# Clears on GpSimd, table writes one by one, and scaling rows with a higher priority in a fused attention and mixture-of-experts kernel

## The chip, the cores and the metric

The kernel runs on one core of a Trainium2 chip. The metric is device time in microseconds (us); a time is that of one execution of the whole program, and where several runs are given, the median counts. The engines have these names in the profile: PE is TensorE (PEld its weight loads), DVE is VectorE, ACT is ScalarE, POOL is GpSimd, SP is SyncE, which here only issues DMAs. POOL also issues the indirect DMAs (gathers and scatters by row index).

## The reference

Causal attention over 4 batches, 8 heads, 576 positions of 64 values, mixed with a read from a memory matrix; its output is the input of a top-2 mixture of 8 experts.

```
scores = causal(scale * q @ k.T);  a = exp(scores - scores.max(-1))
a /= a.sum(-1) + 1e-09
local = a @ v
q_p = phi(q)                                   # phi(x) = max(x,0) + exp(min(x,0))
mem_out = (q_p @ M_prev) / (q_p . z_prev + 1e-06)
g = sigmoid(beta)                              # one per head
x = (g * mem_out + (1 - g) * local)            # rows: (batch, position), 512 columns

noisy_logits = x @ w_gate + log1p(exp(x @ w_noise)) * noise
top2, top2_w = two largest of 8 and their softmax
for e in range(8):  out[mask] += top2_w * (relu(x[mask] @ w1[e]) @ w2[e])     # 1024 hidden
```

## The kernel before

**Attention.** The 576 positions of a batch are cut into five chunks, four of 128 and one of 64; chunk (b, i) is number i of batch b, 20 in all. A chunk is worked off in units (two units of four heads for i < 2, else four of two heads). The main loop runs over the units, `u`, as a pipeline: scores of unit u + 2 (`score`), exponentials of u + 1 (`expo`), transposes of a (`trans`, tile tpa, copied to aT by ScalarE), and the products with v of unit u - 2 (`av`, tile avT). In a unit, the maximum over a row (nb, line 570) is a reduction on VectorE, the exponential (line 591) is on ScalarE. The preparation of later chunks (q and k transposed, split into a high and a low fp32r part on GpSimd, phi of q in qpT, the memory read xm) is slotted in between by a table of due times.

**End of a chunk.** `out_turn` makes the chunk's rows x: VectorE adds 1e-9 to the sums den and multiplies by the gate's denominator (line 659, or 664 for the chunks of 64; tile ar), takes the reciprocal (665), TensorE transposes the attention output xo into tpo (668), VectorE multiplies (670, tile xr) and adds the memory part xm (672). xr is stored to xall_scratch by SyncE (676), and `xt_logits` transposes it (line 153, tile tpx), splits it (xTlh on ScalarE, xTll on VectorE, 158) and multiplies it with the gate weights (165, 166, tile tpl; the logits lg at 173).

**Routing.** When a batch's last chunk is through, `routing` puts some forty small steps (line 199 and around) into the queue `small`, from which the loop takes one between its other steps. It ends with the tile rows, and with ten table writes (`put`, line 285): indirect DMAs on GpSimd that scatter rows to tab_scratch at the slot of each token, ten per batch. They go to the queue `puts`; the loop takes one per unit, two in the last batch. For the third batch (B - 2), `early` stands behind the routing steps as a last one: it drains `puts` at once, loads the first two experts' slots from the table (tabE, line 901, on SyncE, each waiting for all 30 writes) and gathers expert 0's first rows into xgE (three tiles of 128x512 in the buffer xw, line 857). That buffer is the one that held batch 2's keys; `early_rows` takes it over and clears the three tiles by VectorE (line 893). Later `xprep` (line 909) transposes the gathered rows.

**Experts.** From about 283 us on TensorE runs the experts' matmuls (980: ha, hb; 993: y), with weights streamed in and split in high and low parts.

**What sets the order.** A scheduling layer puts the traced instructions of each engine in one static order; `tc.high_priority(offset=n)` makes it place instructions as if they had been traced n steps sooner. `here(f)` traces f behind the last instruction of the step before on VectorE, ScalarE and GpSimd. On the chip each engine works off its order strictly, and waits by semaphores.

Of the kernel before, what the change touches and what calls it, by code (L numbers as in the profile page):

```python
# [15 lines left out]
ALU = mybir.AluOpType  # L16
# [4 lines left out]
B, H, S, D = 4, 8, 576, 64  # L21
# [4 lines left out]
NCH = 5  # L26
# [20 lines left out]
def tile_attention_moe(ctx: ExitStack, tc: tile.TileContext, q, k, v, M_prev, z_prev, beta,  # L47
# [295 lines left out]
    def attention():  # L343
        with ExitStack() as c2:
# [308 lines left out]
            def out_turn(c):  # L653

                d = CH[c]
                n = d["n"]
                r = d["r"] = ap_.tile([P, H], F32, tag="ar", name="ar", bufs=2)
                if d["i"] < 4:
                    nc.vector.scalar_tensor_tensor(out=r, in0=d["den"], scalar=1e-9, in1=il, op0=ALU.add, op1=ALU.mult)
                else:  # L660
                    rv = r[0:n].rearrange("p (g t) -> p g t", t=2)
                    lv = il[0:n].rearrange("p (g t) -> p g t", t=2)
                    for t, s_ in enumerate((d["d2"][0:64], d["xo"][0:64, 0, 64:68])):
                        nc.vector.scalar_tensor_tensor(out=rv[:, :, t], in0=s_, scalar=1e-9, in1=lv[:, :, t], op0=ALU.add, op1=ALU.mult)
                nc.vector.reciprocal(r[0:n], r[0:n])
                tp = ps_tp.tile([P, 512], F32, tag="tp", name="tpo")
                for g in range(4):
                    nc.tensor.transpose(tp[0:n, g * P:(g + 1) * P], d["xo"][:, g, 0:n], ident)
                x_ = d["x"] = rp.tile([P, H, D], F32, tag="xr", name="xr", bufs=3)
                nc.vector.tensor_tensor(out=x_[0:n], in0=tp[0:n].rearrange("p (h e) -> p h e", h=H),  # L670
                                        in1=d["r"][0:n].unsqueeze(2).to_broadcast([n, H, D]), op=ALU.mult)
                nc.vector.tensor_tensor(out=x_[0:n], in0=x_[0:n], in1=d["xm"][0:n], op=ALU.add)
                t0 = d["b"] * S + d["i"] * P

                def keep():
                    nc.sync.dma_start(out=xall[t0:t0 + n, :], in_=x_[0:n].rearrange("p h d -> p (h d)"))
                if c == len(chunks) - 1:
                    R["keep"] = keep
                    return
                keep()  # L680
                xq.extend(xt_logits(d["b"], d["i"], x_.rearrange("p h d -> p (h d)")))
                if d["i"] == 4:
                    xq.append(lambda b=d["b"]: small.extend(routing(b) + ([early] if b == B - 2 else [])))
                if d["b"] == B - 1 and d["i"] == 2:
                    xq.append(lambda: small.extend(routing(B - 1, 0, 3)))
                if d["b"] == B - 1 and d["i"] == 3:
                    xq.insert(1, lambda: xprep(R["XT0"], R["xgE"][0], 0))
                    xq.append(lambda: xprep(R["XT0"], R["xgE"][1], 1))
                    xq.append(lambda: xprep(R["XT0"], R["xgE"][2], 2))
# [81 lines left out]
            def smalls(last=False):  # L771

                for _ in range(2 if last else 1):
                    if small:
                        in_turn(small.popleft())

            for u in range(NU + 2):
                if u + 1 < NU:
                    expo(u + 1)
# [12 lines left out]
                if u < NU:  # L792
# [8 lines left out]
                    if u >= first[len(chunks) - 5] - 2 and splits:  # L801
                        xs.append(lambda f=splits.popleft(): here(f))
                        xs.append(lambda f=splits.popleft(): here(f))
                    if u == first[len(chunks) - 5] + 1:
                        xs.append(lambda: here(early_rows))
                    if chunks[c][1] == 4 and (u + 1 == NU or units[u + 1][0] != c):
                        xs.append(lambda c=c: sums(c))
                    while ev and ev[0][0] < TU[u + 1]:
# [9 lines left out]
                            pops.append(xq.popleft())  # L818
                    if len(xq) > 2:
                        pops.append(xq.popleft())  # L820
                    for _ in range(2 if chunks[c][0] == B - 1 else 1):
                        if puts:
                            xs.append(lambda: puts and here(puts.popleft()))
                    k_ = 0 if c == len(chunks) - 1 else max(0, len(pops) - 1)
                    xs += pops[:k_] + (trans(u) if u > 1 else [])
                    late_ = pops[k_:]
                nx, ny = len(xs), max(1, len(ys))
                done = 0
                late = u >= NU - 4
# [55 lines left out]
    def early_rows():  # L885

        w_ = kp.tile([P, H, S], F32R, tag="kT", name="xw").rearrange("p h s -> p (h s)")
        R["xgE"] = [w_[:, t * DM:(t + 1) * DM].bitcast(F32) for t in range(3)]
        for j in range(2):
            o = 3 * DM + j * 4 * EARLY  # L890
            R["XT0"].append(w_[:, o:o + 4 * EARLY].rearrange("p (c t) -> p c t", c=4))
        for t in range(3):
            nc.vector.memset(R["xgE"][t], 0.0)

    def early():

        while puts:
            puts.popleft()()
        assert len(scat) == 2 * NCH * (B - 1), len(scat)
        for e in range(2):  # L900
            after_puts(nc.sync.dma_start(
                out=tabE[:, e], in_=tab[e * CAP:e * CAP + EARLY].rearrange("(p t) c -> p t c", p=P)))
        for t in range(3):
            gather_x(R["xgE"][t], tabE[:, 0, t, 0:1], (B - 1) * S)
# [392 lines left out]
```

## Time and profile before

| | us |
|---|---|
| median of 3 runs | 735.73 |
| lowest, highest | 734.84, 738.34 |
| the profiled execution, its own time | 733.98 |
| its span, first to last instruction | 732.3 |

| engine | busy, us | share of the span |
|---|---|---|
| PE | 695.3 | 95% |
| PEld | 600.7 | 82% |
| DVE | 459.1 | 63% |
| ACT | 381.3 | 52% |
| POOL | 360.8 | 49% |

The profile is one execution. A timeline row gives the start, the duration, the engine, the line, what is written and read, and in brackets how long the engine had been idle and what ended that. "x8" means eight instructions in one row. A table by stretches gives for each stretch the busy time of each engine and PEclk, the share of full clock that TensorE was granted (1.00 is the upper of two levels, 0.50 the lower). Ends of matmuls are modelled, since they are pipelined.

### The profile page before, as it was taken

How to read it: one execution, taken by the hardware profiler on the slowest of the kernel's cores; microseconds unless marked ns; L12 is line 12 of the kernel's file. 1: busy time of each engine (PE TensorE's matmuls, PEld its weight loads, DVE VectorE, ACT ScalarE, POOL GpSimd, SP SyncE). 2: the span in 40 equal slices, each digit the busy share in tenths (PEclk: the TensorE clock that was granted, in tenths of full speed). 3: DMA queues.
4: the chain of work that ended last, by engine and by line, in shares of the span. 5: the costliest groups of instructions: out<-in, count | busy, mean ns of one | idle time of the engine just before them, and what ended most of it. 6: DMA issues, size and time to landing. Idle time of an engine off the chain costs nothing. (4 is left out here: it accounts for less than half of the span.)

```text
span 732.3 us, 14474 instructions
## 1 busy us (share of the span) xinstructions
PE 695.3 (95%) x5161; PEld 600.7 (82%) x5161; DVE 459.1 (63%) x1097; ACT 381.3 (52%) x963; POOL 360.8 (49%) x378
## 2 busy tenths in 40 slices
PE   7999999999979678999999999999999999999996
PEld 6788878877857567898888898898898898899895
DVE  6767687687877557968785686455454454454322
ACT  5888987878767554444564153153153153253210
POOL 5505325643762534457554676833833753723702
PEclk8999999999989989999999999999999999999999
DMA  8664422432000026769994594693693693753401
GB/s 174 143 155 132 103 59 59 99 89 55 23 10 30 2 75 173 204 180 246 234 248 132 149 238 146 177 215 110 180 211 116 173 227 121 201 151 129 131 1 63
DMA packets 173966, 98.18 MB, mean 134 GB/s; under 512 B 112852, under 2 KB 152276, under 8 KB 173888
## 3 DMA queue, kind: packets, MB, share of 16 engines
q1 hardware_dynamic: 163424, 78.20, 42.6%
q0 software_dynamic: 10080, 18.98, 9.6%
q8 instruction: 42, 0.69, 0.4%
q14 instruction: 36, 0.29, 0.2%
q10 hardware_dynamic: 384, 0.02, 0.0%
HBM read 74.41 MB, written 22.54 MB: 132 GB/s over the span
## 5 line engine op out<-in xcount | busy, mean ns | idle before, releaser
L936 POOL TENSOR_TENSOR w1lm<-w1sm,w1hm 128x512 fp32r<-128x512 f32 x72 | 93.9, 1307 | 121.0 <-DVE w1hm L939 66.5
L993 PE MATMUL y<-w2hm,hTl 128*128 128x512 f32 (+1 forms) x310 | 122.1, 394 | 0.3 <-DVE hTl L984 0.3
L993 PE MATMUL y<-w2hm,hTh 128*128 128x512 f32 (+1 forms) x310 | 122.1, 394 | 0.0
L993 PE MATMUL y<-w2lm,hTh 128*128 128x512 f32 (+1 forms) x310 | 121.4, 392 | 0.0
L983 ACT ACTIVATE hTh<-ha 128x304 fp32r<-128x304 f32 (+2 forms) x64 | 27.2, 424 | 143.0 <-PE ha L980 121.0
L940 DVE TENSOR_TENSOR w2lm<-w2sm,w2hm 128x512 fp32r<-128x512 f32 x74 | 62.2, 841 | 55.8 <-ACT w2hm L939 54.9
L939 ACT CAST w2hm<-w2sm 128x512 fp32r<-128x512 f32 x74 | 45.6, 619 | 95.9 <-PE y L993 83.3
L591 ACT ACTIVATE a<-sc,nb 128x128 f32<-128x128 f32 (+4 forms) x160 | 82.7, 529 | 11.8 <-DVE nb L570 7.4
L570 DVE TENSOR_REDUCE nb<-sc 128x1 f32<-128x384 f32 (+4 forms) x128 | 68.9, 556 | 27.8 <-PE sc L565 11.6
L939 DVE CAST w1hm<-w1sm 128x512 fp32r<-128x512 f32 x74 | 36.1, 488 | 63.3 <-PE hb L980 38.3
L993 PEld LDWEIGHTS y<-w2hm,hTl 128*128 128x128 f32 (+1 forms) x310 | 56.5, 182 | 16.5 <-DVE hTl L984 1.1
L980 PE MATMUL hb<-xTh,w1hm 128*128 128x304 f32 (+2 forms) x224 | 68.6, 306 | 0.2 <-DVE hTl L984 0.2
L980 PE MATMUL ha<-xTl,w1hm 128*128 128x304 f32 (+2 forms) x224 | 68.2, 304 | 0.0
L980 PE MATMUL hb<-xTl,w1hm 128*128 128x304 f32 (+2 forms) x224 | 68.0, 303 | 0.1
L980 PE MATMUL ha<-xTh,w1hm 128*128 128x304 f32 (+2 forms) x224 | 67.8, 303 | 0.0
L980 PE MATMUL hb<-xTh,w1lm 128*128 128x304 f32 (+2 forms) x224 | 67.7, 302 | 0.0
L980 PE MATMUL ha<-xTh,w1lm 128*128 128x304 f32 (+2 forms) x224 | 67.6, 302 | 0.0
L993 PEld LDWEIGHTS y<-w2lm,hTh 128*128 128x128 f32 (+1 forms) x310 | 56.6, 183 | 11.5
L993 PEld LDWEIGHTS y<-w2hm,hTh 128*128 128x128 f32 (+1 forms) x310 | 56.6, 183 | 10.7
L610 ACT COPY aT<-tpa 128x512 f32<-128x512 f32 x120 | 56.6, 518 | 8.4 <-PE tpa L609 4.9
L609 PE MATMUL tpa<-identr,a 128*128 128x128 f32 x400 | 58.9, 281 | 0.8 <-ACT mm L500 0.2
L631 PE MATMUL avT<-aT,vt 128*64 128x128 f32 (+1 forms) x960 | 59.5, 266 | 0.0
(252 smaller groups left out, 1645.9 us busy)
## 6 DMA issues: line engine op xcount, KB each, us to landing
w1sm<-in_moe_w_dram SPq DMA_DIRECT2D x74, 256.0 KB
w2sm<-in_moe_w_dram SPq DMA_DIRECT2D x74, 256.0 KB
y_scratch<-o SPq DMA_DIRECT2D x21, 256.0 KB
vt<-in_v_dram SPq DMA_DIRECT2D x16, 256.0 KB
xall_scratch<-xr SPq DMA_DIRECT2D x16, 256.0 KB
kn<-in_k_dram SPq DMA_DIRECT2D x15, 256.0 KB
qn<-in_q_dram SPq DMA_DIRECT2D x15, 256.0 KB
y_scratch<-o SPq DMA_DIRECT2D x14, 224.0 KB
```

The lines of the kernel that those rows point to most:

```text
L570: R["nb"] = nc.vector.tensor_reduce(out=nb[:, t * nh:(t + 1) * nh], in_=cols[t] if nh == 2 else cols[t][:, 0, :], axis=AX.X, op=ALU.max, n ...
L591: nc.scalar.activation(a[:, o:o + w], s_, AF.Exp, bias=st["nb"][:, x_:x_ + 1], accum_out=d["den"][:, at:at + 1])
L609: nc.tensor.transpose(tp[:, x_ * P:(x_ + 1) * P], a[:, (g + x_) * P:(g + x_ + 1) * P], ident)
L610: nc.scalar.copy(aT[:, g:g + w, :].rearrange("p b t -> p (b t)"), tp[:, 0:w * P])
L631: nc.tensor.matmul(o_[k_ * 64:(k_ + 1) * 64, h0 // 2, 0:n], CH[c0 + j]["v"][:, h0 + k_, :], r_, start=(j == 0), stop=(j == i))
L936: R["w1l"] = lo.tensor_tensor(out=l1, in0=a, in1=h1.bitcast(F32), op=ALU.subtract)
L939: lambda: nc.vector.tensor_copy(h1, a), l1_, lambda: nc.scalar.copy(h2, b_),
L940: lambda: nc.vector.tensor_tensor(out=l2, in0=b_, in1=h2.bitcast(F32), op=ALU.subtract)]
L980: nc.tensor.matmul(o, w_[:, c, :], xT[xi][:, c, c0_ - at:c1_ - at], start=(c == 0 and i_ == 0), stop=(c == 3 and i_ == 2))
L983: R["hh"] = nc.scalar.activation(hT[0][:, c0_:c1_], o, AF.Relu)
L993: nc.tensor.matmul(ys[t][0:b_ - a_], hT[hi][:, a_:b_], w_, start=(f == 0 and i_ == 0), stop=(f == FF // P - 1 and i_ == 2))
```

## The change

Three edits.

1. The clears of the three xgE tiles go from VectorE to GpSimd, and are traced one per unit over three units, beginning with the third unit's step of batch 3 (`clear_row`); the buffer is taken over at the first of them.
2. In `out_turn` the two small rows for ar with the reciprocal, and the product and sum that make xr, stand in `tc.high_priority(offset=240)`, for every chunk.
3. `early` is no longer a step of `small`, and no longer drains the queue. In the last batch each unit takes one table write in the middle of its steps and one at their end, as long as writes of the first three batches are left; `try_early` runs `early` once the thirtieth is traced. The writes of the earlier batches move to another place within the unit.

```diff
-                if d["i"] < 4:
-                    nc.vector.scalar_tensor_tensor(out=r, in0=d["den"], scalar=1e-9, in1=il, op0=ALU.add, op1=ALU.mult)
...
-                nc.vector.reciprocal(r[0:n], r[0:n])
+                with tc.high_priority(offset=240):
+                    if d["i"] < 4:
+                        nc.vector.scalar_tensor_tensor(out=r, in0=d["den"], scalar=1e-9, in1=il, op0=ALU.add, op1=ALU.mult)
...
+                    nc.vector.reciprocal(r[0:n], r[0:n])
...
-                nc.vector.tensor_tensor(out=x_[0:n], in0=tp[0:n].rearrange("p (h e) -> p h e", h=H),
-                                        in1=d["r"][0:n].unsqueeze(2).to_broadcast([n, H, D]), op=ALU.mult)
-                nc.vector.tensor_tensor(out=x_[0:n], in0=x_[0:n], in1=d["xm"][0:n], op=ALU.add)
+                with tc.high_priority(offset=240):
+                    nc.vector.tensor_tensor(out=x_[0:n], in0=tp[0:n].rearrange("p (h e) -> p h e", h=H),
+                                            in1=d["r"][0:n].unsqueeze(2).to_broadcast([n, H, D]), op=ALU.mult)
+                    nc.vector.tensor_tensor(out=x_[0:n], in0=x_[0:n], in1=d["xm"][0:n], op=ALU.add)
...
-                    xq.append(lambda b=d["b"]: small.extend(routing(b) + ([early] if b == B - 2 else [])))
+                    xq.append(lambda b=d["b"]: small.extend(routing(b)))
...
+            def try_early():
+
+                if "early" not in R and len(scat) == 2 * NCH * (B - 1):
+                    R["early"] = True
+                    here(early)
...
-                    if u == first[len(chunks) - 5] + 1:
-                        xs.append(lambda: here(early_rows))
+                    u_ = u - first[len(chunks) - 5] - 2
+                    if u_ == 0:
+                        early_rows()
+                    if 0 <= u_ < 3:
+                        xs.append(lambda t=u_: here(lambda: clear_row(t)))
+                    if len(scat) < 2 * NCH * (B - 1):
+                        xs.append(lambda: puts and here(puts.popleft()))
...
-                    for _ in range(2 if chunks[c][0] == B - 1 else 1):
-                        if puts:
-                            xs.append(lambda: puts and here(puts.popleft()))
...
+                    if chunks[c][0] == B - 1 and "early" not in R:
+                        xs.append(lambda: puts and here(puts.popleft()))
+                        xs.append(try_early)
...
-        for t in range(3):
-            nc.vector.memset(R["xgE"][t], 0.0)
+
+    def clear_row(t):
+        nc.gpsimd.memset(R["xgE"][t], 0.0)
...
-        while puts:
-            puts.popleft()()
```

In the rows of order that follow, the numbers behind the names tell buffers apart and differ between the two programs; the changed kernel's line numbers are larger by 1 to 14 for the same statement (ar 659, 664, 665 become 660, 665, 666; xr 670, 672 become 672, 674; the gather 857 becomes 870).

VectorE, around the end of chunk (2,4): before, from the second maximum of a unit (nb) to the sum that completes xr.

```order
L570 TENSOR_REDUCE nb_3596<-sc_3598 128x2
L940 TENSOR_TENSOR w2lb_2700<-w03_251,w2hb_2699 128x512
L893 MEMSET xw_3628 128x512 x3
L570 TENSOR_REDUCE nb_3673<-sc_3674 128x1
L504 SCALAR_TENSOR_TENSOR mr_3639<-mm_3637,ib_90 128x4
L664 SCALAR_TENSOR_TENSOR ar_3655<-xo_3611,ib_90 64x4
L489 TENSOR_SCALAR qpT_3837<-qf_3694 128x512
L506 RECIPROCAL mr_3639<-mr_3639 128x4
L665 RECIPROCAL ar_3655<-ar_3655 64x8
L670 TENSOR_TENSOR xr_3664<-tpo_3659,ar_3655 64x512
L417 SCALAR_TENSOR_TENSOR qpT_3837<-qf_3694,qpT_3837 128x512
L672 TENSOR_TENSOR xr_3664<-xr_3664,xm_3193 64x512
```

The same place in the changed kernel, from the first maximum of that unit on.

```order
L570 TENSOR_REDUCE nb_3597<-sc_3598 128x2
L665 SCALAR_TENSOR_TENSOR ar_3651<-xo_3612,ib_90 64x4
L952 TENSOR_TENSOR w2lb_2700<-w03_251,w2hb_2699 128x512
L666 RECIPROCAL ar_3651<-ar_3651 64x8
L570 TENSOR_REDUCE nb_3597<-sc_3599 128x2
L672 TENSOR_TENSOR xr_3660<-tpo_3655,ar_3651 64x512
L504 SCALAR_TENSOR_TENSOR mr_3637<-mm_3635,ib_90 128x4
L674 TENSOR_TENSOR xr_3660<-xr_3660,xm_3195 64x512
L660 SCALAR_TENSOR_TENSOR ar_3943<-den_3591,ib_90 128x8
L506 RECIPROCAL mr_3637<-mr_3637 128x4
L570 TENSOR_REDUCE nb_3669<-sc_3670 128x1
L666 RECIPROCAL ar_3943<-ar_3943 128x8
```

The clears are gone from this queue, and the sum that completes xr stands ahead of the next unit's maximum and of both rows of the q work (qpT).

GpSimd, the writes of the third batch's table rows (six_3862), before.

```order
L451 TENSOR_TENSOR kT_3283<-kf_3833,kT_3283 128x4x128
L507 TENSOR_TENSOR xm_3983<-mm_3987,mr_3989 128x256
L507 TENSOR_TENSOR xm_3983<-mm_4060,mr_4062 128x256
L285 DMA tab_scratch<-rows_89,six_3862 19456x4 x10
L857 DMA xw_3628<-xall_scratch,tabE_99 128x512 x3
```

The same in the changed kernel.

```order
L451 TENSOR_TENSOR kT_3285<-kf_3833,kT_3285 128x4x128
L507 TENSOR_TENSOR xm_3991<-mm_3995,mr_3997 128x256
L285 DMA tab_scratch<-rows_89,six_3862 19456x4 x5
L507 TENSOR_TENSOR xm_3991<-mm_4076,mr_4078 128x256
L285 DMA tab_scratch<-rows_89,six_3862 19456x4 x5
L870 DMA xw_3672<-xall_scratch,tabE_99 128x512 x3
```

The ten writes stand in two groups of five, with one row of the memory part between them.

GpSimd, where the clears (L907) stand in the changed kernel.

```order
L507 TENSOR_TENSOR xm_3560<-mm_3635,mr_3637 128x256
L907 MEMSET xw_3672 128x512
L481 CAST qh_3694<-qf_3692 128x512
L907 MEMSET xw_3672 128x512
L483 TENSOR_TENSOR ql_3695<-qf_3692,qh_3694 128x512
L507 TENSOR_TENSOR xm_3754<-mm_3758,mr_3760 128x256
L507 TENSOR_TENSOR xm_3754<-mm_3770,mr_3772 128x256
L907 MEMSET xw_3672 128x512
```

One stands ahead of each of the two rows that split q of a later chunk (qh, ql), the third behind the next two xm rows.

## Rows read from the trace of the kernel before

**Rows 1.** The page's first part: busy time, share of the span, instructions.

```profile
PE 695.3 (95%) x5161; PEld 600.7 (82%) x5161; DVE 459.1 (63%) x1097; ACT 381.3 (52%) x963; POOL 360.8 (49%) x378
```

**Rows 2.** Stretches: start:end length, busy us (instructions) per engine, PEclk, DMA share, GB/s.

```profile
211.10:216.05 4.95, 0.00 (x1) 0.03 (x1) 4.70 (x12) 1.60 (x5) 3.67 (x4) 0.95 0.00 0
216.05:222.40 6.35, 6.35 (x40) 5.27 (x41) 1.05 (x3) 3.22 (x9) 0.68 (x1) 0.50 0.12 23
...
251.30:259.64 8.34, 0.01 (x1) 0.00 (x0) 1.92 (x6) 1.22 (x3) 4.38 (x5) 0.81 0.03 2
259.64:263.40 3.76, 3.76 (x27) 3.23 (x28) 0.00 (x0) 1.52 (x6) 2.06 (x2) 0.51 0.39 105
...
300.00:730.00 430.00, 425.04 (x2426) 377.95 (x2424) 242.45 (x446) 164.44 (x317) 221.53 (x212) 1.00 0.65 166
```

**Rows 3.** Waits of PE on DVE for tpx: us in total, times, longest.

```profile
PE tpx L153 <- DVE ar L659: 5.9, 3, 5.0
```

**Rows 4.** Timeline of PE around 211 us: start, duration, row, idle before.

```profile
210.88 0.22 PE L565 MATMUL sc<-mask,identb 128*128 128x128 bf16 x1
216.05 0.66 PE L153 MATMUL tpx<-identr,xr 64*128 64x64 f32 x4 [4.95 <-DVE ar L659]
...
216.72 1.92 PE L609 MATMUL tpa<-identr,a 128*128 128x128 f32 x8
```

**Rows 5.** Timeline of DVE before 216 us.

```profile
207.66 1.26 DVE L570 TENSOR_REDUCE nb<-sc 128x2 f32<-128x512 f32 x2
209.06 0.69 DVE L940 TENSOR_TENSOR w2lb<-w,w2hb 128x512 fp32r<-128x512 f32 x1
209.81 1.57 DVE L893 MEMSET xw<- 128x512 f32 x3
...
211.77 0.15 DVE L664 SCALAR_TENSOR_TENSOR ar<-xo,ib 64x4 f32<-64x4 f32 x1
...
212.73 0.68 DVE L670 TENSOR_TENSOR xr<-tpo,ar 64x512 f32<-64x512 f32 x1
213.34 1.55 DVE L417 SCALAR_TENSOR_TENSOR qpT<-qf,qpT 128x512 f32<-128x512 f32 x1
214.81 1.09 DVE L672 TENSOR_TENSOR xr<-xr,xm 64x512 f32<-64x512 f32 x1
```

**Rows 6.** Timeline of ACT: the copy of xo.

```profile
208.34 0.17 ACT L644 COPY xo<-avT 64x4 f32<-64x4 f32 x1
```

**Rows 7.** Timelines of PE, ACT and POOL from 244 to 260 us.

```profile
250.24 1.07 PE L609 MATMUL tpa<-identr,a 128*128 128x128 f32 x8
259.64 0.32 PE L165 MATMUL tpl<-xTlh,wgs 128*32 128x128 f32 x1 [8.34 <-ACT aT L610]
...
256.84 0.58 ACT L157 CAST xTlh<-tpx 128x512 fp32r<-128x512 f32 x1 [6.88 <-remote]
...
244.65 1.02 POOL L285 DMA_INDIRECT tab_scratch<-rows,six  x1 [2.64 <-DVE rows L199]
...
256.00 0.90 POOL L285 DMA_INDIRECT tab_scratch<-rows,six  x1 [0.30 <-issue]
```

**Rows 8.** Timelines of ACT and POOL around the six writes at 282 us.

```profile
291.13 0.20 ACT L167 COPY lt<-tpl 32x64 f32<-32x64 f32 x1 [1.41 <-remote]
...
282.15 1.02 POOL L285 DMA_INDIRECT tab_scratch<-rows,six  x1 [5.56 <-DVE ar L665]
...
289.00 0.96 POOL L285 DMA_INDIRECT tab_scratch<-rows,six  x1 [0.30 <-issue]
```

**Rows 9.** PE's row at 275 us, and the stretch around it.

```profile
275.31 0.66 PE L909 MATMUL tpm<-identr,xw 128*128 128x128 f32 x4 [1.16 <-ACT aT L610]
...
270.00:280.00 10.00, 8.01 (x104) 6.35 (x105) 7.21 (x40) 6.09 (x20) 4.82 (x6) 1.00 0.57 176
```

**Rows 10.** POOL: a row after idle time, and the group of its clears (busy, mean ns).

```profile
223.61 1.19 POOL L507 TENSOR_TENSOR xm<-mm,mr 128x256 f32<-128x256 f32 x2 [6.88 <-ACT mm L500]
...
L1059 POOL MEMSET xg<- 128x512 f32 x3 | 1.6, 536 | 5.7 <-PE sc L550 5.3 <-PE tpm L497 0.4
```

More of the change, by code (lines that the diff above doesn't have):

```diff
@@ L657, in out_turn @@
                 r = d["r"] = ap_.tile([P, H], F32, tag="ar", name="ar", bufs=2)
-                if d["i"] < 4:
-                    nc.vector.scalar_tensor_tensor(out=r, in0=d["den"], scalar=1e-9, in1=il, op0=ALU.add, op1=ALU.mult)
[L660 to L664, printed above, removed]
-                nc.vector.reciprocal(r[0:n], r[0:n])
+                with tc.high_priority(offset=240):
+                    if d["i"] < 4:
+                        nc.vector.scalar_tensor_tensor(out=r, in0=d["den"], scalar=1e-9, in1=il, op0=ALU.add, op1=ALU.mult)
+                    else:
+                        rv = r[0:n].rearrange("p (g t) -> p g t", t=2)
+                        lv = il[0:n].rearrange("p (g t) -> p g t", t=2)
+                        for t, s_ in enumerate((d["d2"][0:64], d["xo"][0:64, 0, 64:68])):
+                            nc.vector.scalar_tensor_tensor(out=rv[:, :, t], in0=s_, scalar=1e-9, in1=lv[:, :, t], op0=ALU.add, op1=ALU.mult)
+                    nc.vector.reciprocal(r[0:n], r[0:n])
                 tp = ps_tp.tile([P, 512], F32, tag="tp", name="tpo")
```

## The prediction

> **What bounds the kernel now.** I read the page's busy shares first: TensorE is busy 95% of the span [rows 1], so a change counts by the TensorE time it gives back, not by the work it moves. The table by stretches comes next [rows 2]. From 300 us on, in the expert stage, TensorE is busy 425.04 of 430.00 us at full clock; nothing in the change touches that stage, so what is won before it should carry to the end unless a transfer takes its place. Before that the same table shows two holes: 211.10 to 216.05 (busy 0.00) and 251.30 to 259.64 (busy 0.01). Behind each hole the granted clock is the lower of the two levels: 0.50 over the 6.35 us from 216.05, 0.51 over the 3.76 us from 259.64. The list of TensorE's waits names VectorE for the first hole: transposes into tpx waited 5.9 us in three places, the longest 5.0 [rows 3]. The timelines then say why.
>
> **First hole.** TensorE's last row before it starts at 210.88 and takes 0.22, so TensorE is free at 211.10; tpx starts at 216.05 [rows 4]. It needs the row xr of chunk (2,4), the end of the chain ar, reciprocal, product (line 670), sum (line 672). VectorE works through its queue without a pause: a slice of the weight split (w2lb, 209.06), three clears of xw (209.81, 1.57 us), then maxima, q work and the chain in pieces between them; the sum comes at 214.81, behind a 1.55 us row of the q work [rows 5]. The sources of the chain were ready long before: xo was copied at 208.34 + 0.17 = 208.51 [rows 6].
>
> **Second hole.** TensorE's rows stop at 250.24 + 1.07; the next row, at 259.64, waited 8.34 us for ScalarE. But ScalarE had itself been idle 6.88 us before its row at 256.84, with a releaser the profile cannot name ("remote"). All that time GpSimd issued table writes back to back: ten, the first at 244.65, the last at 256.00, a gap of about 0.30 between them [rows 7]. One more ScalarE wait is put down to "remote" like this, 1.41 us at 291.13, just after a run of six table writes from 282.15 to 289.00 [rows 8]. So a dense run of table writes and this kind of stall stand together twice; that the run causes it is inferred, not shown.
>
> **Edit 1, the clears to GpSimd; edit 2, scaling and row sooner.** Together they rewrite VectorE's queue in front of tpx, as the first pair of order lists shows. I step through the new queue with durations of [rows 5]. The two maxima at 207.66 take 1.26, so the first ends at 208.29. ar waits for xo (208.51) and takes 0.15: 208.66. w2lb cannot start sooner than it did, 209.06, since it waits for ScalarE's cast: it ends at 209.75. The reciprocal, as small a row as ar, 0.15: 209.90. The second maximum 0.63: 210.53. Product 0.68: 211.21. A small mr row 0.15: 211.36. Sum: 0.68 if it is as quick as the product, 1.09 as it was measured: 212.04 to 212.45. TensorE is free at 211.10, so the hole shrinks from 4.95 to between 0.94 and 1.35 us. Gain 3.6 to 4.0; I take 3.9, because the 1.09 was taken beside busy GpSimd work.
> The clock: a hole of 1.16 us stands before 275.31, in a stretch at clock 1.00 [rows 9], while the holes of 4.95 and 8.34 were followed by the lower level [rows 2]. A hole of about 1 us is nearest to the first of these, so I count the drop at 216.05 as gone. What it cost: TensorE was busy all 6.35 us at half rate, so at most 3.2; eight tpa transposes took 1.92 there [rows 4] and 1.07 at full clock [rows 7]. At least nothing, if ScalarE's copies and exponentials (3.22 us busy in the stretch, each waiting for a TensorE result) set the pace instead. I take 1.7, the middle, because both chains run through this stretch.
> The same edit moves the two rows in the other batches by a place or so, ahead of a maximum. The two shorter tpx waits there are 5.9 - 5.0 = 0.9 us together [rows 3]; they can go, or about as much can be lost when a maximum comes 0.7 us later. Gain -0.9 to 0.9, I take 0.3.
> The clears on GpSimd: 536 ns each [rows 10], 1.6 us in all, in front of q's split and the next xm rows. GpSimd idles 6.88 us before 223.61 [rows 10], and the q split there serves chunk (3,3), whose scores come later; so I take 0, and 1.6 lost if that cover fails.
> A rule speaks against this move. [rows 5] show the q row at 213.34 at 1.55 us while GpSimd is at work. The Trainium skill, page "SBUF — State Buffer", section "Who interferes with whom", has it that VectorE and GpSimd share one pair of ports which is held for a whole instruction: a GpSimd instruction that only writes does not hold up a VectorE row with two inputs in SBUF, but copies, casts and single-input arithmetic of VectorE in their two-port modes are shut out by it. By that rule the clears would spare the sum row and could hold three casts or q rows by one clear each, and the gain would be 4.3 instead of 5.9; by the rows above it is 5.9. No row of this trace shows a GpSimd clear beside such a VectorE row.
>
> **Edit 3, the third batch's writes over five units.** The source takes two writes per unit; GpSimd's queue shows something else: five writes, one xm row, five writes. None of them waits for anything but the finished table rows, its own queue's earlier writes and its place, so with issue at 1.26 us apart they will still run as one stretch of about 13 us, broken once. The routing rows on VectorE stand about one unit further ahead than before, so I expect the stretch to begin some 4 us sooner against TensorE's work. That wins nothing by itself: the gathered rows are first used at 275.31, and that wait ended on ScalarE [rows 9]. Behind the writes are queued the loads of tabE on SyncE (with a store of xr behind them) and the three gathers, whose order stays. So the second hole is my disputed term. Bounds: all of it goes, 8.34 + 3.76 / 2 = 10.2 gained; or it grows (third rival). I take 0: the new queue is nearest to the run of ten.
>
> **Sum.** 3.9 + 1.7 + 0.3 = 5.9 us. The profiled execution took 733.98 us (span 732.3, 1.7 around it), which gives 728.1; it lies 1.75 under the median of the runs, 735.73, so against the runs I forecast 735.7 - 5.9 = 729.8. The terms' ends give 3.6 + 0 - 0.9 - 1.6 = 1.1 to 4.0 + 3.2 + 0.9 = 8.1, hence 727.6 to 734.6 for this case alone.
>
> **Rivals.**
> The break heals the second hole. For: a run of six cost ScalarE 1.41 us [rows 8], a run of ten 6.88 and more, so the cost would grow faster than the number, and a run of five may cost little. Two runs of five at 1.4 each, or at twice that, leave 2.8 or 5.6 of the 8.34 us; that and its share of the clock, or all of it gone, gives 4 to 10.2 us on top: 726 to 719.6, middle 723. Against: the break is one row of about 0.6 us.
> The wait only changes its name. The chain gets shorter, but what is next (the exponentials, the q rows now behind it, the next transposes) is late by nearly as much, and the lower clock comes anyway. Then 2 us or less are won: 734. For: VectorE is busy 4.70 of the 4.95 us of the hole [rows 2], and all those rows but the clears must still be done.
> Slower: the writes, now some 4 us sooner, run into the dense softmax work of chunk (3,3), and the stall spans them all: if it began with the first write instead of the fifth (13.0 us, and the 2.7 from the last issue's end, 256.90, to TensorE's 259.64), it would be 15.7 us instead of 8.34, 7.4 more, and with a second stretch at the lower clock, half of 6.35, 3.2 more. 7.4 + 3.2 - 5.9 = 4.7 slower: 740.4. It decides against the change once the second hole exceeds some 14 us.
>
> **How the numbers follow.** Forecast 729.8 with 0.52; second hole healed 0.25; wait renamed 0.15; slower 0.08. Within 0.5% of 735.73 means 732.05 to 739.4, about what a measurement of this kernel can tell from no change. Faster: 0.85 of the forecast, all of the first rival, a little of the second: 0.70. Same: the rest of the forecast (0.07) and most of the second: 0.19. Slower: 0.11, the third rival and mishaps in the second. The range 720 to 735 leaves out about 0.05 below and 0.13 above.
>
> **What would show it.** In the profile of the changed kernel the tpx wait near 211 should be about 1 us, with the clock at 1.00 behind it; if it is over 3 us, step 1 failed. GpSimd should show the clears in idle time, with q's split no later than its scores need it. The ten writes should run as two groups of five within 13 to 14 us, and a hole of 6 us or more on TensorE should end about 2 us behind the last; if that hole is under 3 us, the first rival holds. The expert stage should keep its length. The forecast falls if the second hole moves by more than 3 us either way.

## The result and the profile after

The changed kernel takes 729.0 us (median of 9 runs, 726.0 to 731.1), the kernel before 735.7 us (9 runs, 732.8 to 738.5). The ratio is 0.9912, with a 95% interval of 0.9895 to 0.993: 6.7 us faster. The profiled execution took 729.0 us, its span is 727.2 us, 5.1 us shorter than the 732.3 of before.

The first hole. Stretches of the changed kernel, with the columns of [rows 2]; the first is TensorE's wait for tpx, the second runs from there to the transpose tpL of line 171:

```profile
209.25:210.03 0.78, 0.01 (x2) 0.03 (x1) 0.78 (x4) 0.78 (x4) 0.00 (x0) 1.00 0.03 1
210.03:216.04 6.01, 5.83 (x57) 4.91 (x58) 4.39 (x13) 5.33 (x15) 4.58 (x7) 1.00 0.11 25
```

The wait of 4.95 us [rows 4] is 0.78 us, and the clock behind it is 1.00 where it was 0.50 [rows 2]. TensorE's timeline gives the distance from tpx to the same tpL row in both kernels; first before:

```profile
224.30 0.27 PE L171 MATMUL tpL<-identr,lt 128*64 128x128 f32 x1
```

and after, with the tpx row:

```profile
210.03 0.43 PE L153 MATMUL tpx<-identr,xr 64*128 64x64 f32 x4 [0.78 <-DVE ar L660]
216.04 0.27 PE L171 MATMUL tpL<-identr,lt 128*64 128x128 f32 x1
```

From tpx to tpL it is 224.30 - 216.05 = 8.25 us before and 6.01 us after. VectorE's timeline of the changed kernel (compare [rows 5]):

```profile
206.69 0.60 DVE L665 SCALAR_TENSOR_TENSOR ar<-xo,ib 64x4 f32<-64x4 f32 x1 [0.80 <-ACT xo L644]
...
207.82 0.19 DVE L666 RECIPROCAL ar<-ar 64x8 f32<-64x8 f32 x1
...
208.49 0.67 DVE L672 TENSOR_TENSOR xr<-tpo,ar 64x512 f32<-64x512 f32 x1
...
209.20 0.68 DVE L674 TENSOR_TENSOR xr<-xr,xm 64x512 f32<-64x512 f32 x1
```

Scaling, product and sum now follow each other with one split row, one maximum and one mr row between them; the chain ends at 209.88.

The second hole. Timelines of GpSimd, ScalarE and TensorE of the changed kernel (compare [rows 7]); of each five writes the first and the last stand here:

```profile
231.76 1.04 POOL L285 DMA_INDIRECT tab_scratch<-rows,six  x1 [3.08 <-DVE qpT L489]
...
236.93 0.97 POOL L285 DMA_INDIRECT tab_scratch<-rows,six  x1 [0.30 <-issue]
237.92 0.62 POOL L507 TENSOR_TENSOR xm<-mm,mr 128x256 f32<-128x256 f32 x1
238.71 1.01 POOL L285 DMA_INDIRECT tab_scratch<-rows,six  x1 [0.17 <-issue]
...
243.79 0.91 POOL L285 DMA_INDIRECT tab_scratch<-rows,six  x1 [0.30 <-issue]
```

```profile
244.75 0.58 ACT L642 COPY xo<-avT 128x512 f32<-128x512 f32 x1 [3.82 <-remote]
```

```profile
237.50 0.46 PE L436 MATMUL tpk<-identr,kn 64*128 64x64 f32 x4 [0.43 <-issue]
239.64 1.09 PE L609 MATMUL tpa<-identr,a 128*128 128x128 f32 x8 [1.52 <-issue]
246.69 1.12 PE L669 MATMUL tpo<-identr,xo 128*128 128x128 f32 x4 [5.90 <-ACT kf L443]
```

The three waits are 0.43 + 1.52 + 5.90 = 7.85 us, against 8.34 before. TensorE goes on 1.99 us behind the last write (243.79 + 0.91 = 244.70). The stretches around it, and a later one at the lower clock:

```profile
237.07:246.69 9.62, 1.77 (x15) 1.34 (x15) 1.19 (x3) 3.30 (x9) 6.22 (x7) 0.75 0.03 2
246.69:252.10 5.41, 5.41 (x31) 4.73 (x32) 3.25 (x8) 2.70 (x7) 2.85 (x3) 0.50 0.33 84
...
269.20:272.70 3.50, 3.22 (x36) 2.54 (x35) 1.38 (x9) 0.99 (x3) 0.00 (x0) 0.51 0.78 272
```

The expert stage starts in the changed kernel at

```profile
276.88 0.44 PE L992 MATMUL ha<-xw,w1ha 128*128 128x384 f32 x1 [0.68 <-issue]
```

and at 283.29 in the kernel before. So the changed kernel is 8.26 us ahead at tpL (224.30 - 216.04), 6.41 us at the expert stage (283.29 - 276.88), and 5.1 us at the end.

### The profile page after: what moved, and what is told of

It is laid out like the page before. It is cut to its first block, busy times and chain, and to the rows that moved or that the text cites. A ratio compares the mean times of both kernels' runs of the same rounds, so it can differ in the third digit from the quotient of the medians.

```text
span 727.2 us, 14473 instructions
## 1 busy us (share of the span) xinstructions
PE 696.2 (96%) x5161; PEld 599.7 (82%) x5161; DVE 459.6 (63%) x1094; ACT 381.3 (52%) x963; POOL 361.1 (50%) x381
## 5 line engine op out<-in xcount | busy, mean ns | idle before, releaser
L952 DVE TENSOR_TENSOR w2lm<-w2sm,w2hm 128x512 fp32r<-128x512 f32 x74 | 65.3, 883 | 55.0 <-ACT w2hm L951 53.2
L609 PE MATMUL tpa<-identr,a 128*128 128x128 f32 x400 | 57.3, 278 | 1.8 <-issue 1.5
```

What stands on the lines that cost most here:

```text
L609: nc.tensor.transpose(tp[:, x_ * P:(x_ + 1) * P], a[:, (g + x_) * P:(g + x_ + 1) * P], ident)
L952: lambda: nc.vector.tensor_tensor(out=l2, in0=b_, in1=h2.bitcast(F32), op=ALU.subtract)]
```

## Experiments

Beside the runs of the result three chips were used, one for each set of four kernels, and each set was timed against the kernel before on its own chip. There the kernel before took 735.1 us on the first chip, 735.9 us on the second, and 727.6 us on the third (17 runs each).

| kernel | chip | median us | ratio to before, 95% interval |
|---|---|---|---|
| edit 1 alone | 1 | 728.9 | 0.9916 (0.9893 to 0.994) |
| edit 2 alone | 1 | 730.7 | 0.993 (0.9902 to 0.9957) |
| edit 3 alone | 1 | 735.1 | 0.9992 (0.9968 to 1.0015) |
| changed, writes paced by unit | 1 | 724.3 | 0.9859 (0.9836 to 0.9883) |
| changed, third batch's writes left out | 2 | 718.5 | 0.9761 (0.9717 to 0.9806) |
| changed, writes doubled | 2 | 741.2 | 1.0064 (1.0034 to 1.0093) |
| changed, one clear between writes | 2 | 721.3 | 0.9804 (0.9757 to 0.9851) |
| changed, two clears between writes | 2 | 725.7 | 0.9862 (0.9819 to 0.9905) |
| changed, clear of 256 between writes | 3 | 719.8 | 0.9889 (0.9871 to 0.9907) |
| changed, clear of 384 between writes | 3 | 720.1 | 0.9913 (0.9886 to 0.9939) |
| before, one clear between writes | 3 | 728.4 | 1.0018 (1.0003 to 1.0034) |
| changed, writes of 64 rows | 3 | 716.3 | 0.9839 (0.982 to 0.9857) |

### One edit at a time

Edit 1 alone, the kernel before with

```diff
-        for t in range(3):
-            nc.vector.memset(R["xgE"][t], 0.0)
+    def clear_row(t):
+        nc.gpsimd.memset(R["xgE"][t], 0.0)
```

> The kernel before with edit 1 alone: the three clears on GpSimd, one per unit; VectorE's other rows in the order of before, the third batch's ten writes untouched. The theory of the forecast (the wait for tpx near 211 us is set by VectorE's queue): the clears took 1.57 us of that queue, so the wait of 4.95 us shrinks to about 3.4 us, the stretch behind it still shows the lower clock, and the time falls by about 1.6 us (0.2%). Rival (the order of the small rows alone sets the wait): the wait stays near 5 us and the time is that of before. A rule of shared ports by which the clears would hold up VectorE: casts or q rows beside a clear 0.5 us longer, and under 1 us won.

It won 0.84%, some 6.2 us: not the 1.6 us of the theory, and no rival. Its TensorE timeline, the stretch 205:225 and its VectorE timeline:

```profile
210.14 0.43 PE L153 MATMUL tpx<-identr,xr 64*128 64x64 f32 x4 [1.22 <-DVE xr L672]
```

A stretch of it:

```profile
205.00:225.00 20.00, 18.01 (x185) 14.28 (x187) 17.48 (x51) 17.04 (x55) 9.88 (x13) 1.00 0.08 22
```

```profile
208.31 0.19 DVE L665 RECIPROCAL ar<-ar 64x8 f32<-64x8 f32 x1
...
208.59 0.68 DVE L670 TENSOR_TENSOR xr<-tpo,ar 64x512 f32<-64x512 f32 x1
209.31 0.68 DVE L672 TENSOR_TENSOR xr<-xr,xm 64x512 f32<-64x512 f32 x1
```

In the kernel before the reciprocal, product and sum stood behind the clears and then had maxima and q work between them [rows 5]. With the clears gone from VectorE's list the order around them changed too: product and sum stand right behind the reciprocals, and the q row of line 417, 1.55 us before the sum in [rows 5], comes behind it. The expectation kept the old order and took away 1.57 us; that was its error.

Edit 2 alone, the kernel before with

```diff
+                with tc.high_priority(offset=240):
...
+                    nc.vector.reciprocal(r[0:n], r[0:n])
...
+                with tc.high_priority(offset=240):
...
+                    nc.vector.tensor_tensor(out=x_[0:n], in0=x_[0:n], in1=d["xm"][0:n], op=ALU.add)
```

> The kernel before with edit 2 alone: scaling and row instructions of each chunk sooner on VectorE; the clears stay on VectorE where they stood, the ten writes untouched. The theory of the forecast: of the 4.95 us wait near 211 us about 1 to 2.5 us are left, depending on whether the clears still stand ahead of the reciprocal; the lower clock behind it goes, and the shorter waits for tpx and tpo in the other batches shrink by some 0.3 us each: 3 to 5.5 us won, so nearly the whole gain of the change. Rival (edit 1 is what matters): under 2 us won and the wait stays over 3 us.

It won 0.70%, 4.4 us, within its range of time. The wait for tpx is 0.70 us, under the 1 to 2.5 us expected, and the clock behind it is 1.00:

```profile
210.70 0.43 PE L153 MATMUL tpx<-identr,xr 64*128 64x64 f32 x4 [0.70 <-DVE xr L674]
```

A stretch of it:

```profile
205.00:225.00 20.00, 18.16 (x187) 14.46 (x187) 17.63 (x56) 17.58 (x55) 9.50 (x12) 1.00 0.08 22
```

The clears still run on VectorE here, one between product and sum (209.52, 0.48 us) and two behind the chain (212.38). So edits 1 and 2 are two ways to the same 4 us: each alone closes the hole, and from the start of the wait for tpx to tpL it takes 13.20 us before, 7.20 with edit 1, 6.56 with edit 2 and 6.79 with all three. In time the whole change wins no more than either (0.9912, inside both intervals). The two together without edit 3 were not run.

Edit 3 alone, the kernel before with

```diff
-                    for _ in range(2 if chunks[c][0] == B - 1 else 1):
-                        if puts:
-                            xs.append(lambda: puts and here(puts.popleft()))
+                    if len(scat) < 2 * NCH * (B - 1):
+                        xs.append(lambda: puts and here(puts.popleft()))
...
+                    if chunks[c][0] == B - 1 and "early" not in R:
+                        xs.append(lambda: puts and here(puts.popleft()))
+                        xs.append(try_early)
```

> The kernel before with edit 3 alone: the third batch's writes over more units and the early loads behind them; clears and small rows as before. The theory of the forecast: the wait near 211 us stays at about 5 us, the long hole behind the writes stays (6 to 8.5 us, some 7 to 14 us sooner against the span), time within 1 us of before. Rival (the gain of the change came from the writes): 3 us or more won without a shorter wait near 211 us.

No change in time (the interval leaves room for 2.4 us faster to 1.1 us slower). The first hole is there in full, clock included, and the second has the shape that it has in the changed kernel:

```profile
214.25 0.66 PE L153 MATMUL tpx<-identr,xr 64*128 64x64 f32 x4 [4.96 <-DVE ar L659]
252.53 1.12 PE L668 MATMUL tpo<-identr,xo 128*128 128x128 f32 x4 [5.28 <-ACT kf L443]
```

A stretch of it:

```profile
205.00:225.00 20.00, 15.04 (x138) 12.30 (x135) 13.82 (x37) 13.25 (x43) 8.10 (x11) 0.83 0.08 21
```

### What makes the second hole

Writes paced by unit: the changed kernel, and ahead of each unit's first write in the last batch

```diff
+            def gate(u):
+                if u + 1 in U:
+                    nc.gpsimd.tensor_copy(gt[:, 0:2], U[u + 1]["nb"][:, 0:2])
...
+                        if chunks[c][0] == B - 1:
+                            xs.append(lambda u=u: puts and here(lambda: gate(u)))
```

> The changed kernel with the third batch's writes really spread: ahead of each unit's first write GpSimd copies two numbers out of the next unit's bias, so that the writes of a unit wait for it and the run of ten becomes pairs about 5 us apart. Theory A (a dense run of table writes on GpSimd makes TensorE's results visible late and so makes the second hole): the hole of 5.90 us and the two shorter waits before it go, with most of the 10.2 us at the lower clock: 6 to 11 us sooner than the changed kernel, 718 to 723 us. Theory B (the hole is another thing that stands there, such as the routing or the transfers behind the writes): a hole of 5 us or more stays near 240 us or moves with those transfers, and the time is within 2 us of the changed kernel's 729. Theory C (the dense run delays results only while a profile is taken): the hole is gone from the profile, but the time without a profile is that of the changed kernel.

It took 724.3 us, 0.9859 of before; the changed kernel has 0.9912. The pacing took only from the eighth write on: seven came together from 230.44 to 239.73, the others at 244.14, 247.93 and 254.28. What is left of the hole:

```profile
236.88 0.46 PE L437 MATMUL tpk<-identr,kn 64*128 64x64 f32 x4 [0.91 <-issue]
241.57 1.11 PE L670 MATMUL tpo<-identr,xo 128*128 128x128 f32 x4 [2.81 <-ACT kf L444]
263.25 0.63 PE L928 MATMUL tpm<-identr,xw 128*128 128x128 f32 x4 [2.68 <-DMA xw<-xall_scratch,tabE]
```

3.72 us are left of 7.85, and 2.68 us come new, because the gathers stand behind the last write. The time lies 1.3 us above theory A's range of 718 to 723 us, in its direction.

Third batch's writes left out:

```diff
         def put(i, w):
+            if b == B - 2:
+                skipped.append(1)
+                return
```

> The changed kernel without the third batch's ten table writes; so the table lacks that batch's rows and the early gathers take other rows, and nothing else is left out. Theory A (the dense run of writes makes the second hole): the holes between 237 and 252 us (7.85 us of waits) and the 10.2 us at the lower clock go; against the changed kernel 7.85 + up to 5.1 = 8 to 13 us sooner, 716 to 721 us. Theory B (something else stands there, such as the routing on VectorE, the loads of tabE or the stores behind them): a hole of 5 us or more stays, and the time stays within 2 us of 729.

718.5 us, as theory A has it. Without the writes no wait over 0.7 us is left from 225 to 255 us, and the clock is 1.00:

```profile
225.00:255.00 30.00, 28.44 (x299) 23.58 (x299) 21.88 (x90) 23.49 (x66) 7.12 (x9) 1.00 0.13 40
```

The loads, the gathers and the routing on VectorE are still there, so theory B falls for this chip.

Writes doubled:

```diff
+            if b == B - 2:
+                s2 = nc.gpsimd.indirect_dma_start(
+                    out=tab2, out_offset=bass.IndirectOffsetOnAxis(ap=six[0:n, i - c0, w:w + 1], axis=0),
+                    in_=rows[0:n, b, i, w, :], in_offset=None)
```

> The changed kernel with each of the third batch's ten writes issued a second time, into a second table that nobody reads: a run of twenty, some 25 us long. Theory A: TensorE's results come late for as long as the run lasts and about 2 us beyond it, so the waits grow from 7.85 us by about the 12.6 us of the ten added writes, 739 to 745 us. Theory A2 (only a fixed price is paid, at the end of a run, such as one queue that has to drain): the waits grow by under 4 us, 729 to 733. Theory B: no change but for the gathers 12.6 us later, up to 735.

741.2 us, as theory A has it. Twenty writes run from 229.82 to 255.42, with TensorE's waits and a stretch at the lower clock:

```profile
236.28 0.66 PE L618 MATMUL tpa<-identr,a 128*128 128x128 f32 x4 [0.73 <-issue]
244.02 1.12 PE L678 MATMUL tpo<-identr,xo 128*128 128x128 f32 x4 [6.00 <-issue]
259.07 1.09 PE L155 MATMUL tpx<-identr,xr 128*128 128x128 f32 x4 [10.29 <-DVE ar L669]
```

A stretch of it:

```profile
243.00:262.00 19.00, 7.70 (x42) 6.63 (x43) 4.39 (x10) 4.69 (x11) 9.47 (x10) 0.50 0.07 16
```

The waits sum to 17.0 us, 9.2 us more than the changed kernel's 7.85, for ten more writes; 12.6 us more were expected, so the time came out right with fewer waits than theory A asked for. They go on for as long as the run does and a little beyond (259.07, against 255.42).

One and two clears between the writes:

```diff
+                if b == B - 2 and "wr" in R:
+                    for _ in range(1):
+                        sp_.enter_context(tc.issue_after(R["wr"]))
+                        R["wr"] = nc.gpsimd.memset(gt, 0.0).ins
+                    sp_.enter_context(tc.issue_after(R["wr"]))
```

> The changed kernel with one clear of a 128x512 scratch tile (about 0.54 us) held between each two of the third batch's writes on GpSimd: issue about 1.9 us apart instead of 1.27, the run some 18 us long, gathers 5 us later. Theory A with a rate (writes pile up when they come faster than they are worked off, in about the 2.6 us that one write waits behind the next in the paced kernel's result): waits shrink in part, 724 to 728 us. Theory A with a number (ten writes in a row, at any spacing under some 4 us): the waits grow with the run to 10 us or more, 730 to 735. If the hole is gone altogether, the writes are worked off within 1.9 us each: 718 to 723.

> As the kernel with one clear between the writes, with two: issue about 2.4 to 2.5 us apart, the run 23 us long, gathers 10 us later, so that TensorE waits some 3 us for the first gathered rows, as in the paced kernel (2.68 us). Theory A with a rate: no wait over 1 us is left inside the run, the lower clock does not come behind it, 722 to 726 us with the wait for the gathers. Theory A with a number: a hole at least as long as with one clear, 730 us or more.

With one clear 721.3 us, with two 725.7 us. GpSimd's timeline with one clear, the stretch 225:255, and the wait behind:

```profile
235.47 0.98 POOL L292 DMA_INDIRECT tab_scratch<-rows,six  x1 [0.17 <-issue]
236.45 0.54 POOL L290 MEMSET gt<- 128x512 f32 x1
237.15 0.98 POOL L292 DMA_INDIRECT tab_scratch<-rows,six  x1 [0.17 <-issue]
```

A stretch of it:

```profile
225.00:255.00 30.00, 28.80 (x302) 23.74 (x298) 22.38 (x91) 23.21 (x66) 17.01 (x22) 1.00 0.07 20
```

and TensorE's wait behind it:

```profile
258.05 0.63 PE L930 MATMUL tpm<-identr,xw 128*128 128x128 f32 x4 [2.35 <-DMA xw<-xall_scratch,tabE]
```

The same ten writes, 1.68 instead of 1.27 us apart, make no hole at all: TensorE is busy 28.80 of these 30 us, as it is without the writes (28.44). So ten writes alone do not make the hole; it takes their spacing, and 0.41 us more between two writes is enough on this chip. With two clears (2.26 us apart) the hole stays away as well, but the gathers come 5 us later still, and TensorE waits for them 8.26 us instead of 2.35, more than the 3 us expected (in the profiled execution, at 728.2 us the longest of its six):

```profile
263.87 1.09 PE L930 MATMUL tpm<-identr,xw 128*128 128x128 f32 x4 [8.26 <-DMA xw<-xall_scratch,tabE]
```

### Smaller spacings, and a chip that seems not to pay for the hole

The last four kernels ran on the third chip: the changed kernel with a smaller clear, the kernel before with a full clear, and the changed kernel with half the rows per write.

```diff
-                        R["wr"] = nc.gpsimd.memset(gt, 0.0).ins
+                        R["wr"] = nc.gpsimd.memset(gt[:, 0:256], 0.0).ins
```

> As the kernel with one clear between the third batch's writes, with a clear of half the size (128x256, some 0.27 us): issue about 1.42 us apart, between the 1.27 that made the hole and the 1.68 that did not. Theory of the rate, with what a write takes to be worked off read from the runs of ten and twenty (TensorE moves again some 14.3 to 14.9 us after a run of ten began, 28 us after a run of twenty: 1.4 to 1.5 us a write): the backlog stays under 1 us, no hole over 2 us, the gathers come 2.6 us sooner than with the full clear and TensorE's wait of 2.35 us for them goes: 717 to 721 us. Rival (a limit near 1.6 us): a hole of 2 to 5 us comes back, 722 to 727.

> As before, with a clear of 128x384 (some 0.4 us), issue about 1.55 us apart: no hole behind the writes by either limit, the gathers 1.2 us sooner than with the full clear, the wait for them about 1.1 us instead of 2.35 and the lower clock behind it possibly gone: 717 to 721.5 us, against 721.3 with the full clear.

719.8 and 720.1 us, with writes 1.47 and 1.57 us apart; the wait for the gathered rows is gone with the first and 2.90 us with the second, where 1.1 us was expected.

The kernel before with the full clear (the diff of one clear above, in the old put), and the last one:

> The kernel before, without any of the three edits, with one full clear between the third batch's ten writes. If the two holes are independent, as the sum of the forecast takes them, the hole of 8.34 us and its lower clock go and the one of 4.95 us near 211 us stays: 7.5 to 10 us sooner than before, 726 to 728.5 us, and 6 to 7 us behind the changed kernel with the same clears. Rival (the first hole is made good for by the second, so that they overlap): within 2 us of 721.

```diff
-            n = rows_of(i)
+            n = 64 if b == B - 2 else rows_of(i)
```

> The changed kernel with the third batch's ten writes of 64 table rows each instead of 128 (the last two had 64 already), back to back as they were; the other half of that batch's table rows is left out. If a write's price behind the queue goes by its rows, about 0.7 us are left, less than the 0.9 plus 0.3 us from issue to issue, and the holes go: 716 to 721 us. If it goes by the write, the waits stay near 7.85 us and the time near 729.

The kernel before with the clear took 728.4 us, close to the 726 to 728.5 expected. But there is no gain in it: the kernel before itself takes 727.6 us on this chip, 8 us less than on the other two. Its trace with the clear shows the first hole in full, no second hole, and a wait for the gathers:

```profile
215.57 0.66 PE L154 MATMUL tpx<-identr,xr 64*128 64x64 f32 x4 [4.94 <-DVE ar L668]
268.67 1.09 PE L918 MATMUL tpm<-identr,xw 128*128 128x128 f32 x4 [4.92 <-DMA xw<-xall_scratch,tabE]
```

A stretch of it:

```profile
225.00:255.00 30.00, 28.57 (x289) 22.72 (x286) 22.70 (x82) 22.76 (x64) 13.48 (x18) 1.00 0.08 28
```

Its expert stage runs from 277.51 to the span's end in 451.3 us (449.0 in the kernel before), and the first hole is there. Only the stretch of the second hole is left to hold the 8 us, so the run of ten writes seems to cost this chip little or nothing. That is inferred: no trace of an unspaced run of ten full writes was taken there, and the changed kernel itself was not run there, so what the clears win over it on this chip is not known. It takes from the four runs what they were meant to tell: where between 1.27 and 1.68 us the limit lies, and whether a write's price goes by its rows (716.3 us fits, but on this chip it proves nothing), stay open. So does whether the holes add up.

## Why the prediction was right, point by point

**First hole: right, a little too long.** Forecast 0.94 to 1.35 us, measured 0.78. The gain is 4.95 - 0.78 = 4.2 us for 3.9. The sum row took 0.68 us, the lower of the two values weighed; GpSimd ran nothing beside it (idle from 208.73 to 210.19). What the working missed is that the two edits are substitutes: it stepped through a queue with both, and the runs of one edit each show that either does it.

**Clock behind it: right, middle too small.** The drop is gone. From tpx to tpL 8.25 - 6.01 = 2.2 us were won; the term was 1.7 (0 to 3.2).

**The other batches: too small, and for the most part another edit's.** TensorE reaches the wait at 209.25 instead of 211.10, so 1.85 us were won earlier, for a forecast of 0.3 (-0.9 to 0.9). The forecast gave this term to edit 2 alone and let edit 3 win nothing by itself; edit 3 also moves the earlier batches' writes, and that had no term. From the first tpL of the span (39.76 us before, 39.30 after) to the start of the wait for tpx it takes 171.34 us before, 171.34 with edit 1 alone, 170.78 with edit 2, 169.88 with edit 3 and 169.95 with all three: some 0.6 us from edit 2 and 1.5 from edit 3, by one trace each. The waits agree. Those for tpx fell from 0.47 to 0.18 us, and do so with edit 2 alone; two of those for tpo fell from 0.65 and 0.76 to 0.25 and 0.26, and do so with edit 3 alone. The second of these, with edit 2 alone, then with edit 3 alone:

```profile
159.42 0.63 PE L669 MATMUL tpo<-identr,xo 128*128 128x128 f32 x4 [0.77 <-DVE M L223]
```

```profile
158.99 0.63 PE L668 MATMUL tpo<-identr,xo 128*128 128x128 f32 x4 [0.27 <-DVE eq L199]
```

One wait before 206.68 grew by 0.56. The other 0.46 us lie ahead of the first tpL, which stands anywhere between 37.58 us (edit 1 alone) and 39.76 us (the kernel before) in the traces. These two begin with the same rows in the same order and differ in TensorE's clock (0.78 before and 1.00 with edit 1 from 4 to 10 us, 0.74 and 1.00 from there to 17 us), so this part is chance.

**Clears on GpSimd: right.** They stand at 210.74, 211.97 and 216.50 us; q's split ends at 214.08, and no wait of TensorE for it shows near there. On the rule of shared ports in the Trainium skill (page "SBUF — State Buffer", section "Who interferes with whom") the rows do speak now. VectorE's single-input q row and its two-input q row, and GpSimd's clears beside them (the second clear, at 211.97, took 0.52 us):

```profile
210.53 1.03 DVE L489 TENSOR_SCALAR qpT<-qf 128x512 f32<-128x512 f32 x1
...
212.27 0.67 DVE L417 SCALAR_TENSOR_TENSOR qpT<-qf,qpT 128x512 f32<-128x512 f32 x1
```

```profile
210.74 0.53 POOL L907 MEMSET xw<- 128x512 f32 x1
```

The single-input row with nothing of GpSimd beside it (edit 2 alone):

```profile
213.34 0.41 DVE L489 TENSOR_SCALAR qpT<-qf 128x512 f32<-128x512 f32 x1
```

The two-input row kept 0.67 us beside a clear, as the rule has it for a GpSimd instruction that only writes; before, beside rows of GpSimd that read two inputs, it took 1.55 us [rows 5]. The single-input row is 0.62 us longer, about one clear, which fits the rule; but it began 0.21 us ahead of the clear, while an xm row of GpSimd still ran (210.19 to 210.80), and with edit 1 alone it took 0.72 us beside the end of a table write and a cast, without a clear. So the clear's share of the 0.62 us is not shown. The row stands behind the chain, so the 1.6 us that the rule would have cost did not come.

**Writes and second hole: right in place and size, not in what follows.** Five writes, an xm row, five writes in 12.9 us (13 to 14 forecast); TensorE goes on 1.99 us behind the last (about 2 forecast); 7.85 us of waits for 8.34. The writes begin 15.72 us behind tpL instead of 20.35, so 4.6 us sooner (some 4 forecast). But the term of 0 was too high. From tpL to the expert stage 8.26 - 6.41 = 1.85 us were given back, though the waits in the hole are 0.5 us shorter. The rows for it are the stretches at the lower clock: in the kernel before TensorE was at the lower level for 3.76 us behind the hole [rows 2], in the changed kernel for 5.41 us, and again for 3.50 us from 269.20, behind a wait of 1.11 us that is about as long as the one of 1.16 us which the clock survived before [rows 9]. Half of 5.41 + 3.22 - 3.76 = 4.9 us of busy time is 2.4 us, about the 1.85 us given back and the 0.5 us together. Edit 3 is not the cause by itself: this way takes 58.99 us before, 58.91 with edit 3 alone, 60.75 with edit 1 and 63.23 with edit 2, where TensorE was at the lower level in three stretches. Why TensorE is busy longer at the lower level in these kernels stays open.

**Expert stage: 1.3 us longer** (276.88 to 727.2, against 283.29 to 732.3), where no change was forecast. Two waits at 338.71 and 339.87 us, 0.64 and 0.42 us for hTh and hTl, are 1.1 of it. In the traces of all kernels this stage takes 448.8 to 455.0 us, though no edit touches it, so the 1.3 us may be chance.

So the mechanism of the first hole held, and the sum came out close by luck, because its errors cancel: 0.3 + 0.5 + 1.5 us more won before tpL than forecast, 1.85 + 1.3 us lost behind it. Profile 5.1 us, runs 6.7 us, forecast 5.9.

**The rivals.** "The wait changes its name" and "slower" fell with the rows of the first hole and the 7.85 us. "The break heals the second hole" fell too: one xm row of 0.62 us, in one of nine gaps, left 7.85 us of waits, while a clear in each gap left none. The guess behind it, that a dense run of writes and the stall belong together, was inferred in the forecast and is now shown on the second chip, by leaving the writes out, doubling them and spacing them.

## What to carry to other kernels

A wait caused by the order of one engine's queue can have several cures that do not add up; time each alone before counting both. Spreading work over more units in the source does not spread it on an engine whose rows become ready late and all at once: read the issue times in the engine's own timeline, and pace them there if the rate matters. Here a clear of 0.54 us between two table writes won about as much again as the whole change on the second chip (0.9804 of before; the changed kernel, in the runs of the result, 0.9912). On the third chip the kernels with smaller clears are at 0.9889 and 0.9913 of before, about what the change alone won elsewhere. And compare positions in two traces from a common row on: the same code, ahead of the first tpL, ended up to 2.2 us apart.

## What the runs showed of the hardware

Back-to-back indirect writes from GpSimd, 1.27 us apart, hold up TensorE, ScalarE and VectorE together in the traces of the result and on the first two chips (in the changed kernel waits of 5.90, 3.82 and 6.46 us end between 244.7 and 246.7), though the DMA engines are almost idle meanwhile (share 0.03 in the stretch 237.07:246.69). Ten writes gave 7.85 us of waits of TensorE, twenty 17.0 us, ten at 1.68 us apart none. By what path they do it was not found. On the third chip the kernel before is 8 us quicker, ten writes of 64 rows 1.2 us apart made no hole, and no wait is put down to "remote" in the four traces; none of them has ten full writes unspaced. The profiles' pages differ there in one more thing: the third chip's record landing times of the transfers, of the table writes too, the others' none. The line of the kernel with the clear of 256, then that of the changed kernel:

```profile
tab_scratch<-rows,six POOLq DMA_INDIRECT x40, 2.8
```

```profile
tab_scratch<-rows,six POOLq DMA_INDIRECT x40
```

Spans and granted clocks are recorded for the timed runs as well. So whether the stall belongs to the chips, or to how executions are recorded on them (theory C in a wider form), stays open.

TensorE's clock does not follow the length of the last wait alone: behind 2.68 us it stayed at 1.00 (writes paced by unit, 263.25 to 270.00), behind 2.35 us it fell (one clear; 0.57 from 258 to 264 us). A wait of 1.16 us left it at 1.00 in the kernel before [rows 9]; with edit 2 alone one of 1.16 us at 268.09 was followed by 0.50 from 270 us on. The stretches of the first two:

```profile
263.25:270.00 6.75, 5.16 (x89) 4.18 (x89) 3.59 (x21) 2.34 (x6) 4.49 (x6) 1.00 0.86 283
```

```profile
258.00:264.00 6.00, 5.33 (x47) 3.99 (x47) 2.61 (x15) 1.70 (x4) 4.88 (x7) 0.57 0.89 299
```
